# Transposing raw x before its layer norm, and pairing two triples of score banks, in a pre-LN transformer block

## The chip, the cores and the metric

The kernel runs on one core of a Trainium2 chip. The metric is the device time of one execution in microseconds (us). The engines are TensorE (PE in the profile, its weight loads PEld), VectorE (DVE), ScalarE (ACT), GpSimd (POOL) and the DMA queue that SyncE (SP) feeds.

## The reference

One block for 2048 tokens of width 640, in bf16, with 32 heads of 20 and a gated feed-forward of 1728:

```
def _layernorm(x, axis=-1, eps=1e-5):
    m = jnp.mean(x, axis=axis, keepdims=True)
    v = jnp.var(x, axis=axis, keepdims=True)
    return (x - m) / jnp.sqrt(v + eps)
...
qkv = (x @ wqkv) split into q, k, v of 32 heads x 20
p = softmax(q k^T * 20 ** -0.5);  A_ref = (p v) @ wo
B_ref = (gelu(x @ w_gate) * (x @ w_up)) @ w_down
h = x + A_ref(_layernorm(x));  out = h + B_ref(_layernorm(h))
```

## The kernel before

**Planner.** The program is a list of operations made by `op(engine, instructions, duration, priority, ...)`. `Sched.schedule` plays them through with the given durations and fixes the order of each engine's instructions: among the operations that are ready, the lowest priority number goes first. PSUM has eight banks; an operation that starts a chain acquires one of an allowed set, and the one that empties it releases it. The tuples at the head of the file (QK_LEAD, PE_AGE, SD_AGE and others) steer the choice for PE, one number for each slot. Most instructions carry line 450, that of a helper.

**First stage.** x comes in four loads of 512 tokens, then the weights of Q, K and V. Statistics for tiles 0 to 10 (128 tokens each) come from bn_stats on DVE (`ln_stats`), for tiles 11 to 15 from sums on ACT (`act_stats`). `ln_rsqrt` makes 1/std, `ln_apply` on DVE the normalised tile, PE transposes it (L675), and ACT or DVE copies it to `xnT` (L681, L684). From `xnT` come K and Q of the first 128 channels (`proj_k(0)`, `proj_q(0, 0)`, products at L758, copies at L795 and L800), and V (`proj_v`, L907, copies at L917). The maximum of |K| (`km`, L792) scales a bound on the scores (`sel0`, `q_bound0`), which Q carries as an extra row. Scores can be formed from then on. The other channels of K, Q and V are projected as background in the first slots (copies at L803).

**Attention.** Queries are cut into chunks of 512, 256 (five times) and 128 (twice): `CHUNKS`. A slot is one PSUM bank of output: one group of four heads for 512 queries, two groups for 256, four for 128. That is 32 slots: 0 to 7 for chunk 0, four each for chunks 1 to 5, two each for chunks 6 and 7. A slot has 64 score tiles of 128 x 512 numbers. Most go through the exponential on ACT, in units of two or three tiles: scores in banks 0 to 2, then in 3 and 4, and so on in turn, each unit one ACT instruction of 1024 or 1536 columns into `pts` or the part of `rege` called `pts2`. D_SLOT[s] x 4 tiles of slot s go to DVE: a quad is four conversions from PSUM (L992) and four steps over 2048 columns, whose four terms PE adds up in the P x V product; SUMS says how many pairs of terms DVE adds itself instead. A DVE tile either rides in the third bank of a unit (D_RING says how often; that unit then has two ACT tiles) or has a score matmul of its own and one of the background banks. P x V accumulates in bank 6. DVE copies it out at a slot's end (`epilogue`). Where PE would be idle the planner adds products with zeros (`pad`, `warm`).

**Background.** `post(c)` (output projection, layer norm, feed-forward of chunk c) runs beside the attention of the later chunks, in the banks of `BG` (7 and 5 before); its evacuations are L1285, L1373, L1379, L1390 and L1410. What is left after the last exponential, with chunk 7's own `post`, is the tail.

## Time and profile before

| what | us |
|---|---|
| median of three runs | 867.64 (867.41 to 868.66) |
| span of the profiled execution | 866.0 |
| its own time | not given apart from the span |
| first exponential starts | 32.84 |
| last exponential ends | about 841.5 |

The span runs from the first to the last instruction of the core; a run's time is a little longer. In the page's rows "xN" counts instructions, "busy" is the time in which an engine has any of them in work, and the mean duration of one contains its overlap with the next. The rows that matter are shown in the prediction.

### The profile page before, as it was taken

The page shows a single profiled execution, that of the slowest core. Times are in us where ns is not written, and L with a number is a line of the kernel's source. Part 1 is how long each engine was busy: PE and PEld are TensorE (multiplying, and loading weights), DVE is VectorE, ACT ScalarE, POOL GpSimd, SP SyncE. Part 2 cuts the span into 40 slices and gives each one's busy share as a digit, 9 for nine tenths or more (in the row PEclk, how much of TensorE's full clock was granted, in tenths as well). Part 3 has the DMA queues.
Part 4 walks back from the last instruction along what each step waited for, and adds up shares of the span by engine and source line. Part 5 has one row for each costly group of instructions (what it writes and reads, how often), then busy time and mean ns, then how long its engine had stood idle before and what let it go on. Part 6 is the DMA issues. An engine that isn't in the chain of part 4 may idle for free.

```text
span 866.0 us, 35545 instructions
## 1 busy us (share of the span) xinstructions
PE 838.5 (97%) x16215; PEld 420.4 (49%) x16215; DVE 750.4 (87%) x1372; ACT 838.4 (97%) x806; POOL 89.6 (10%) x268
## 2 busy tenths in 40 slices
...
GB/s 274 81 47 61 29 76 47 59 61 92 58 16 60 160 147 80 16 18 36 53 42 16 36 8 61 5 35 17 49 19 24 58 12 27 20 47 11 2 18 17
DMA packets 50173, 43.19 MB, mean 50 GB/s; under 512 B 21316, under 2 KB 44640, under 8 KB 50024
## 3 DMA queue, kind: packets, MB, share of 16 engines
...
q8 instruction: 127, 2.08, 1.0%
q14 instruction: 22, 0.18, 0.1%
...
## 4 chain that ended last, share of the span: by engine, by line
ACT 51%; PE 39%; DVE 8%; issue 1%
ACT pts L450 35%; ACT rege L450 15%; PE ps L1081 11%; PE ps L450 10%; PE ps L753 9%; PE ps L758 3%; DVE qt_all L450 2%; DVE rege L450 2%; PE ps L907 1%; PE ps L1336 1%; DVE rege L992 1%; DVE qt_all L992 1%; PE ps L1405 1%; ACT qt_all L450 1%; PE ps L675 1%
## 5 line engine op out<-in xcount | busy, mean ns | idle before, releaser
L450 ACT ACTIVATE pts<-ps 128x1024 bf16<-128x1024 f32 (+1 forms) x496 | 558.5, 1240 | 2.8 <-PE ps L1081 2.2
L1081 PE MATMUL ps<-qt_all,kt_all 32*128 32x256 bf16 (+2 forms) x4096 | 304.0, 273 | 11.5 <-ACT pts L450 5.6
L450 ACT ACTIVATE rege<-ps 128x1024 bf16<-128x1024 f32 (+1 forms) x222 | 248.3, 1199 | 0.7 <-PE ps L1081 0.3
L1081 PEld LDWEIGHTS ps<-qt_all,kt_all 32*128 32x128 bf16 x4096 | 103.2, 92 | 202.8 <-ACT pts L450 90.6
L992 DVE TENSOR_SCALAR rege<-ps 128x512 int16<-128x512 f32 x220 | 148.5, 684 | 20.0 <-PE ps L1081 18.6
L450 PE MATMUL ps<-rege,v_all 128*21 128x256 bf16 (+2 forms) x2197 | 139.3, 286 | 0.5 <-DVE rege L450 0.5
L450 PE MATMUL ps<-pts,v_all 128*21 128x256 bf16 (+2 forms) x2403 | 124.8, 273 | 1.0 <-DVE osb L450 0.8
L753 PE MATMUL ps<-rege,regw 128*32 128x256 bf16 (+1 forms) x2600 | 120.5, 296 | 1.6 <-DVE rege L992 0.5
L992 DVE TENSOR_SCALAR qt_all<-ps 128x512 int16<-128x512 f32 x128 | 86.7, 683 | 11.0 <-PE ps L1081 10.2
L450 DVE TENSOR_SCALAR rege<-rege 128x2048 int16<-128x2048 int16 x141 | 94.5, 687 | 1.5 <-PE ps L450 0.8
L753 PEld LDWEIGHTS ps<-rege,regw 128*32 128x32 bf16 x2600 | 60.4, 96 | 34.6 <-issue 20.1
L450 PEld LDWEIGHTS ps<-rege,v_all 128*21 128x21 bf16 x2197 | 54.4, 91 | 41.6 <-issue 26.1
L450 PEld LDWEIGHTS ps<-pts,v_all 128*21 128x21 bf16 x2403 | 56.6, 91 | 26.0 <-issue 19.2
L450 DVE TENSOR_SCALAR qt_all<-qt_all 128x2048 int16<-128x2048 int16 (+4 forms) x113 | 65.4, 589 | 3.0 <-ACT qt_all L450 1.0
L753 PE MATMUL ps<-regw,rege 128*32 128x320 bf16 x1296 | 67.4, 301 | 0.3 <-DVE rege L992 0.3
L758 PE MATMUL ps<-regw 128*128 128x512 bf16 (+2 forms) x215 | 59.6, 368 | 0.4
L450 PE MATMUL ps<-qt_all,v_all 128*21 128x256 bf16 (+1 forms) x1264 | 56.5, 264 | 0.8 <-DVE qt_all L450 0.8
L450 DVE TENSOR_SCALAR qt_all<-rege 128x2048 int16<-128x2048 int16 x80 | 53.8, 684 | 1.6 <-PE ps L450 1.2
L450 POOL TENSOR_SCALAR rn<-rc 128x16 int32<-128x16 int32 x22 | 7.0, 317 | 461.7 <-DMA rc<-sums 461.6
L1390 DVE TENSOR_TENSOR rege<-rege,ps 128x512 bf16<-128x512 bf16 (+2 forms) x53 | 35.0, 661 | 13.0 <-PE ps L753 6.6
L1336 PE MATMUL ps<-rege,regw 128*128 128x128 bf16 (+1 forms) x420 | 40.9, 238 | 0.0
L753 PEld LDWEIGHTS ps<-regw,rege 128*32 128x32 bf16 x1296 | 30.0, 96 | 18.3 <-issue 10.8
...
## 6 DMA issues: line engine op xcount, KB each, us to landing
...
```

The costliest lines, as they stand in the source:

```text
L450: return lambda eng: getattr(eng, method)(*args, **kwargs)
L675: op("pe", lambda eng, a=a: eng.transpose(bank16(bk, D)[:, 128 * a:128 * a + 128], src[:, a * 128:(a + 1) * 128], ident[:]), 0.055, prio, ...
L753: return [lambda eng, j=j: eng.matmul(out()[32 * j:32 * j + 32], l[:, 32 * j:32 * j + 32], r, start=start, stop=stop, tile_position=(0, 32 ...
L758: fn = col4(lambda: bank(bk, n), l, r, k == 0, k == len(steps) - 1) if col else lambda eng, l=l, r=r, k=k: eng.matmul(bank(bk, n), l, r, s ...
L907: w_readers.append(op("pe", lambda eng, i=i, kt=kt, a=a: eng.matmul(bank(bk)[:, i * w:i * w + w], xnT[:, a, kt * 128:(kt + 1) * 128], wv[: ...
L992: d_ops.append(op("dve", lambda eng: eng.tensor_scalar(v[:, 512 * h:512 * h + 512], bank(b), EXP_MUL, -32000.0, ALU.mult, ALU.max), c_dve( ...
L1081: return lambda eng: eng.matmul(out()[:, kk * nq:(kk + 1) * nq], kt_all[32 * j:32 * j + 32, g, kt * 128:(kt + 1) * 128], qt_all[32 * j:32 ...
L1336: lambda eng, a=a, f=f, fi=fi: eng.matmul(bank(bk)[:, fi * nq:(fi + 1) * nq], w[:, a, F0[f]:F0[f] + 128], hnT[:, a, 128 * tb:128 * tb + nq ...
L1390: hdone.append(op("dve", lambda eng, bu=bu, fv=fv, w=w: eng.tensor_tensor(fv, fv, bank(bu, w), ALU.mult), c_dve(w), p, reads=[ku] + hkeys( ...
L1405: f == NF - 1) if cl else lambda eng, f=f, o=o, bk=bk, w0=w0, w1=w1: eng.matmul(
```

## The change

**First stage.** x is transposed as it arrives (`xT`, which has a column of ones behind each 128 tokens). The mean is taken out of the weights: a matmul with ones gives the column sums, ACT copies them scaled by 1/640, POOL or DVE (CM_DVE) subtracts them (`center`); the weights are loaded in slices, the first 128 columns of K and of Q between the sets of x. 1/std is put on the products. For the first channels of K and Q (`proj_t0`) the product is formed with tokens on the partitions, scaled there by `rs`, and transposed back; the other K and Q products are multiplied on DVE with a broadcast of 1/std (`make_r`, buffers `rb`), V with `rs`. Tiles outside BN get their mean and squares from a Gram product of the transposed tile: the last column and the diagonal. `act_stats` and the normalised tiles of the first stage are gone.

**Attention.** Chunks 2 to 5 (slots 12 to 27) pair banks 0 to 2 with banks 3 to 5. P x V takes bank 6 or 7 in turn, and BG is what is left of 7, 6, 5 and 4. DVE tiles of the next slot may come up to eight ahead (AHEAD). D_SLOT, SUMS, D_RING, D_SPAN and D_FIRST get other numbers. The planner's costs for changing the PE's tiling are given for each pair of modes, and its tuples for each slot are other numbers.

```diff
-D_SLOT = (1,) + (3,) * 26 + (2, 3, 3, 0, 0,)
-SUMS = (0,) + (1,) * 4 + (2, 2, 0, 0, 1, 0,) + (1,) * 3 + (0, 1, 1, 2, 3, 1, 0, 1, 1, 0, 2, 2, 1, 0, 1, 0, 3, 0,)
+D_SLOT = (2,) + (3,) * 27 + (4, 2, 0, 0,)
+SUMS = (2, 1, 1, 1,) + (0,) * 5 + (1, 0, 1, 1,) + (0,) * 8 + (2, 1, 0, 0, 1, 1,) + (0,) * 5
...
+TOK_DVE = ((False, 0, 0), (False, 1, 0), (False, 1, 1), (False, 3, 0), (True, 0, 0), (True, 1, 1), (True, 2, 0), (True, 2, 1), (True, 3, 0), (True, 3, 1))
+CM_HOLD = 1
+CM_DVE = (('wk', 2), ('wk', 4), ('wq', 4), ('wv', 1), ('wv', 2))
...
-D_RING = (9,) * 4 + (6, 6,) + (9,) * 6 + (6,) * 16 + (12,) + (6,) * 3
-D_FIRST = 0
-D_SPAN = (16,) + (18,) * 13 + (17,) + (18,) * 4 + (19,) * 4 + (18,) * 7 + (17, 17,)
-D0 = 8
-P33 = ()
...
+D_RING = (12, 9, 9, 9, 3,) + (9,) * 4 + (6, 6, 6, 12, 24,) + (12,) * 9 + (9, 12, 24, 9, 9, 9, 6, 3, 9,)
...
+PVB, BGB = (6, 7), (7, 6, 5, 4)
+D_FIRST = (8,) + (0,) * 7 + (-2,) + (0,) * 10 + (2, 0, 0, -2, 2,) + (0,) * 6 + (1, 1,)
+AHEAD = 2
+D_SPAN = (15, 18, 17,) + (18,) * 9 + (17, 16, 18, 17, 17, 17, 18, 17, 18, 17, 17, 17, 19, 17, 17, 17, 18, 22, 22, 15,)
+P33 = (2, 3, 4, 5)
...
+LORD = ('x0', 'k', 'x1', 'q', 'x2', 'x3')
+RAW_DVE = (7, 9)
...
+BN = (0, 1, 2, 3, 7, 8, 10, 11, 12, 15)
...
-GROUPS = ((0, 4), (4, 7), (11, 5))
+GROUPS = ((0, 4), (4, 8), (12, 4))
...
+        def center(w, lo, hi, cm, ckeys, lkey, parts, prio):
...
+                    op("pe", lambda eng, a=a, a0=a0, bk=bk, n_=n_: eng.matmul(
+                        bank(bk, n_), one[:, 0:1].to_broadcast([128, 128]), w[:, a, lo + a0:lo + a0 + n_], start=a == 0, stop=a == NA - 1),
+                       c_mm(n_), prio, mode="full", reads=[lkey, "one"], writes=[key], acq=[bk] if a == 0 else [])
...
+                eng = "dve" if wkey in CM_DVE else POOL
+                op(eng, I("tensor_tensor", w[:, :, lo + a0:lo + a1], w[:, :, lo + a0:lo + a1],
+                          cm[:, a0:a1].unsqueeze(1).to_broadcast([128, NA, a1 - a0]), ALU.subtract),
...
+        center(wqk, D, D + 128, cm_t0[:, 0:128], [("bs", j) for j in range(4)], "lk0", [(0, 128, ("wk", 0))], P_K0)
+        center(wqk, 0, 128, cm_t0[:, 128:256], [("bs", j) for j in range(4)], "lq0", [(0, 128, ("wq", 0))], P_K0)
+        for t in range(NT):
+            transposes(x_sb[:, t, :], [f"x{t // 4}"], xT[:, :, t, 0:128], ("xnT", t), ALLB, P_TR, "dve" if t in RAW_DVE else "act")
+            e_ops.append(len(sc.ops) - 2)
...
+                    op("pe", lambda eng, i=i, t=t, a=a, bk=bk: eng.matmul(
+                        bank(bk)[:, 129 * i:129 * i + 129], xT[:, a, t, 0:128], xT[:, a, t, 0:129], start=a == 0, stop=a == NA - 1),
+                       c_mm(129), P_GR, mode="full", reads=[("xnT", t), "xones"], writes=[key], acq=[bk] if i == a == 0 else [])
...
+                op("dve", lambda eng, i=i, t=t, bk=bk: eng.scalar_tensor_tensor(
+                    out=junk[t % 8], in0=bank(bk)[:, 129 * i:129 * i + 128], scalar=1.0, in1=ident[:], op0=ALU.mult, op1=ALU.mult,
+                    accum_out=ssq[:, t:t + 1]), 0.25, P_RS, reads=[key, "ident"], writes=[("junk", t % 8), ("ssq", t)], rel=[bk] if i == n - 1 else [])
+        for t in BN:
+            ln_stats(x_sb[:, t, :], t, [f"x{t // 4}"], P_RS)
         for t0, n in GROUPS:
-            if (t0, n) == AG:
-                act_stats(t0, n)
-            else:
-                for t in range(t0, t0 + n):
-                    ln_stats(x_sb[:, t, :], t, [f"x{t // 4}"], P_BG)
-            ln_rsqrt(t0, n, P_RS, sqrt=True)
...
-                e_ops.append(ln_apply("dve", x_sb[:, t, :], xn_p[:, t % 4, :], ("xnp", t % 4), t, [f"x{t // 4}"], P_PRO))
...
+            op("act", I("activation", sl(mu), mv[:, t0:t0 + n, 1], ACT.Sqrt, bias=eps[:]), 0.2, 1, reads=k("mv") + ["eps"], writes=k("mu"))
+            v(I("reciprocal", sl(rs), sl(mu)), k("mu"), k("rs"))
+
+        def make_r():
...
+                        op("pe", lambda eng, i=i, src=src, name=name, bk=bk: eng.matmul(
+                            bank(bk)[:, 128 * i:128 * i + 128], src.to_broadcast([128, 128]), ident[:], start=name == "rhi", stop=name == "rlo"),
+                           c_mm(128), P_R, mode="full", reads=[name, "ident"], writes=[key], acq=[bk] if i == 0 and name == "rhi" else [])
+                fn = lambda eng, c=c, bk=bk: eng.activation(rb[c], bank(bk), ACT.Copy) if R_ENG == "act" else eng.tensor_copy(rb[c], bank(bk))
+                op(R_ENG, fn, c_act(512) if R_ENG == "act" else c_dve(512), P_R, reads=[key],
+                   writes=[("R", c)], rel=[bk], after=tuple(e_ops[0:8]) if c < 3 else ())
...
+            w_readers.append(op("dve", lambda eng: eng.tensor_tensor(dst, bank(bk), rb[c], ALU.mult), c_dve(512), prio,
+                                reads=[key, ("R", c)] + rb_home[c], writes=[dkey], rel=[bk], after=after))
+        def proj_t0(col, c, dst, dkey, banks, prio):
+            isk = col > 0
+            buf, home = (ktok, ("da", 0)) if isk else (qtok, "ka")
+            for p in range(2):
...
+                if (isk, c, p) in TOK_DVE:
+                    op("dve", lambda eng, bk=bk, ts=ts: eng.tensor_tensor(
+                        buf[:, ts[0]:ts[0] + 2, :], bank(bk, 256).rearrange("p (t s) -> p t s", t=2),
+                        rs[:, ts[0]:ts[0] + 2].unsqueeze(2).to_broadcast([128, 2, 128]), ALU.mult), c_dve(256), prio,
...
+                op("pe", lambda eng, i=i, t=t: eng.transpose(bank16(bk, 512)[:, 128 * i:128 * i + 128], buf[:, t, :], ident[:]), 0.055, prio - 0.005,
+                   mode="full", reads=[("tok", isk, t), "ident", home], writes=[key], acq=[bk] if i == 0 else [])
...
+            rv = rs[:, kts[0]:kts[0] + n].unsqueeze(2).unsqueeze(3).to_broadcast([128, n, 4 * (g1 - g0), DH])
+            w_readers.append(op("dve", lambda eng: eng.tensor_tensor(dst, src(), rv, ALU.mult), c_dve(n * w), prio,
+                                reads=[key] + [("rs", kt) for kt in kts], writes=wr, rel=[bk], after=after))
...
-            want = min(nd, (k[0] - first) * nd // (D_SPAN[s_] if isinstance(D_SPAN, tuple) else D_SPAN) + 1) if k[0] >= first and nd else 0
...
+                for t, k in ((s_, in_slot[s_]), (s_ + 1, in_slot[s_] - n_units[s_])):
+                    if t == len(slots) or not d_rem[t]:
+                        continue
+                    nd = 4 * len(d_kb[t])
+                    i = d_used[t]
+                    if k >= d_first[t] + i * D_SPAN[t] / nd - 1e-6 and i < nd and (t == s_ or i < 4 * AHEAD):
+                        xd = d_rem[t].pop(0)
+                        d_used[t] += 1
+                        ring[-1] = n == 3 and (i + 1) * D_RING[t] // nd > i * D_RING[t] // nd
+                    break
+                n -= ring[-1]
...
+            if not pv_ops:
+                pv_ops.append(Bank(*PVB))
+            bk = pv_ops[0]
...
-        BG = [tuple(b for b in (7, 5, 4) if b not in PAT[c][0] + PAT[c][1]) for c in range(len(CHUNKS))]
+        BG = [tuple(b for b in BGB if b not in PAT[c][0] + PAT[c][1]) for c in range(len(CHUNKS))]
```

408 lines of the change are left out of this document (246 added, 162 removed).

## The prediction

> **What bounds the kernel now.** I read the page first, then the busy time by stage, then ScalarE's instructions by shape, then the chain of waits.
>
> ```profile
> span 866.0 us, 35545 instructions
> PE 838.5 (97%) x16215; PEld 420.4 (49%) x16215; DVE 750.4 (87%) x1372; ACT 838.4 (97%) x806; POOL 89.6 (10%) x268
> 0.00:32.80 32.80, 26.96 (x242) 20.37 (x242) 27.61 (x82) 25.25 (x47) 11.71 (x31) 0.95 0.53 193
> 32.80:228.00 195.20, 190.85 (x1733) 62.50 (x1732) 174.04 (x297) 193.97 (x181) 19.36 (x61) 1.00 0.22 63
> 529.70:629.00 99.30, 97.81 (x2449) 54.44 (x2444) 98.61 (x183) 99.15 (x95) 10.97 (x32) 1.00 0.11 30
> 730.30:841.50 111.20, 109.12 (x2888) 72.16 (x2880) 75.63 (x152) 109.98 (x103) 3.77 (x14) 1.00 0.10 22
> 841.50:866.00 24.50, 21.66 (x298) 18.14 (x295) 11.77 (x32) 7.93 (x15) 0.00 (x0) 1.00 0.04 15
> ```
>
> In the stage rows the busy times stand in the order PE, PEld, DVE, ACT, POOL. There are three stretches: a first stage of 32.8 us, the attention from 32.8 to 841.5 us in which ACT is busy nearly all the time, and 24.5 us of tail. PE looks as busy as ACT, but its score matmuls wait for ACT to give banks back, so ACT sets the pace:
>
> ```profile
> PEld ps L1081 <- ACT pts L450: 90.6, 281, 0.9
> ```
>
> What ACT does there, by shape:
>
> ```profile
> L450 ACT ACTIVATE pts<-ps 128x1024 bf16<-128x1024 f32 x300 | 308.2, 1073 | 0.9 <-PE ps L1081 0.6
> L450 ACT ACTIVATE pts<-ps 128x1536 bf16<-128x1536 f32 x196 | 293.0, 1495 | 1.9 <-PE ps L1081 1.6
> L450 ACT ACTIVATE rege<-ps 128x1024 bf16<-128x1024 f32 x154 | 156.8, 1070 | 0.1
> L450 ACT ACTIVATE rege<-ps 128x1536 bf16<-128x1536 f32 x68 | 101.4, 1491 | 0.6 <-PE ps L1081 0.3
> L450 ACT ACTIVATE qt_all<-qt_all 128x1024 f16<-128x1024 f16 x13 | 14.3, 1112 | 0.0
> L450 ACT ACT_TABLE_LOAD x8 | 10.3, 1283 | 0.9 <-PEq L1508 0.8
> L450 ACT ACTIVATE rege<-rege 128x2048 bf16<-128x2048 bf16 x4 | 7.4, 1902 | 0.0
> ```
>
> So 454 exponentials cover two score tiles (1024 columns) and 264 cover three: 1700 tiles. Their records overlap, so the price of one is its spacing, which the chain shows:
>
> ```profile
> 276.87 2.75 ACT rege L450 x3
> 279.62 5.44 ACT pts L450 x5
> ```
>
> The first row is three of 1024 columns, 0.917 us each. The second is three of 1024 and two of 1536, so one of 1536 takes (5.44 - 2.75) / 2 = 1.345, say 1.344. That is 0.427 us for a tile and 0.063 for an instruction. All exponentials: 454 x 0.917 + 264 x 1.344 = 771.1 us. The Gelu and Tanh rows, smaller shapes of both and four of the table loads add about 30 us. Of the 808.7 us from 32.8 to 841.5 some 8 us are left: gaps between exponentials, all that better timing could win.
>
> **Part 1: fewer and wider exponentials.** I worked through the loop over `units` with the diff's tuples: a slot has 64 tiles, 4 x D_SLOT of them go to DVE, and a unit takes 3, then 2 tiles (3, then 3 in slots 12 to 27), one less if a DVE tile rides in its third bank. With the old tuples the loop gives 454 and 264, as the rows show. With the new ones it gives 411 and 290: 1692 tiles, as D_SLOT sums to 89 instead of 87. Time: 411 x 0.917 + 290 x 1.344 = 766.6 us, that is **-4.5 us**: slot 0 gives 1.7, slots 1 to 11 0.4, slots 12 to 27 1.8, the last four 0.6. The 17 instructions fewer are 1.1 us of it, the 8 tiles 3.4. The wide third bank is thus mostly spent on the DVE tiles that ride (183 of 192 in slots 12 to 27, 49 before), not on wider exponentials.
>
> **Part 2: what DVE and PE pay for it.**
>
> ```profile
> L992 DVE TENSOR_SCALAR rege<-ps 128x512 int16<-128x512 f32 x220 | 148.5, 684 | 20.0 <-PE ps L1081 18.6
> L450 DVE TENSOR_SCALAR rege<-rege 128x2048 int16<-128x2048 int16 x141 | 94.5, 687 | 1.5 <-PE ps L450 0.8
> L450 DVE TENSOR_TENSOR qt_all<-qt_all 128x2048 bf16<-128x2048 bf16 x9 | 10.9, 1213 | 0.0
> 136.33 0.40 PE ps L1081 x3
> 140.16 0.97 PE ps L450 x16
> ```
>
> A DVE quad is four of the first and four of the second: 5.5 us. Two more: +11 us. SUMS asks for 13 pair sums instead of 28, each the third row: -18.2 us. DVE is eased by some 7 us over the attention. PE gets what the sums saved: 15 quads of P x V plus 3 x 2 for the new DVE quads, 21 quads at 0.24 us (the last row is 16 matmuls, four quads, in 0.97 us), +5 us. Against that 127 DVE tiles no longer need a score matmul and a bank of their own (348 - 95 = 253 before, 356 - 230 = 126 after). No row prices such a lone tile. The nearest is a whole unit (the L1081 row: three tiles at a time in 0.40 us), so it saves between nothing and 127 x 0.4 = 50 us; I take 0.2 us, 25 us over 16 slots. PE is eased too. As neither sets the end, I count only the gaps: of 8 us they could give back 4, and with a DVE that must now empty the third bank in time they could grow by 6. I take -1.
>
> **Part 3: the first stage.** This is the part with many terms.
>
> ```profile
> 11.63 0.16 DVE L450 RECIPROCAL rs<-sd 128x4 f32<-128x4 bf16 x1
> 30.51 0.16 DVE L450 TENSOR_REDUCE kd<-km 128x1 f32<-128x5 f32 x1
> 32.84 5.97 ACT pts L450 x5
> L450 DVE BATCH_NORM_STATS2 stats<-rege 128x6 f32<-128x320 bf16 x22 | 9.3, 455 | 0.0
> L450 DVE TENSOR_SCALAR rege<-rege,mu,rs 128x640 bf16<-128x640 bf16 x16 | 7.4, 497 | 0.3 <-PE ps L675 0.2
> L450 DVE BATCH_NORM_AGGREGATE mv<-stats 128x2 f32<-128x12 f32 x11 | 2.1, 194 | 0.1
> L684 DVE COPY regw<-ps 128x640 bf16<-128x640 bf16 x4 | 2.0, 489 | 0.4 <-PE ps L675 0.2
> L792 DVE TENSOR_REDUCE km<-ps 128x1 f32<-128x128 f32 x1 | 0.3, 280 | 0.0
> L1225 DVE CAST rege<-ps 128x256 bf16<-128x256 f32 x5 | 2.1, 418 | 0.0
> L681 ACT ACTIVATE regw<-ps 128x640 bf16<-128x640 bf16 x12 | 7.9, 718 | 1.0 <-PE ps L675 1.0
> L450 ACT ACTIVATE rege<-rege 128x640 bf16<-128x640 bf16 x10 | 7.3, 734 | 1.4 <-DMA rege<-in_A_x_dram 1.3
> ```
>
> The first exponential starts 2.3 us after the maximum over K is complete, and that link (kd, sel0, the bound, the first scores) stays. Ahead of it DVE is the busiest engine: 27.6 of 32.8 us, of which the first 6.5 us hold only fills. From DVE go 16 normalisations (7.4), one of eleven tiles of bn_stats with its aggregate (0.9), two of the four transpose copies (1.0), and the casts and small steps of `act_stats` and `ln_rsqrt` (about 12 at 0.15, 1.8): -11.1 busy. To it come six Gram diagonals (nearest row the 128-column reduction from PSUM, 0.28: 1.7), three means and nine small steps (0.15 each: 1.8), and seven scaled products of 256 columns (0.42: 2.9), with two steps for `make_r` (0.3): +6.7. Net -4.4 us busy. ACT loses ten passes for sums (7.3, and their accumulator reads) and gains two copies more (1.4), small products (about 1.5) and four copies of R (4 x 0.6): it stays below DVE. What follows the last statistics is one scaled product, a transpose and the reduction instead of normalise, transpose, copy, product and reduction, so it is no longer than before.
>
> The other bounds are arrivals. SP issues three loads more, all at the front; behind them in its queue come only the copies of Q and K, which wait for products, so nothing there is late. The last set of x comes behind two slices of 160 KB of weights, 0.4 us each at the 395 GB/s of the load, and the centring of those slices is a new step on POOL.
>
> ```profile
> GB/s 0 0 72 184 322 392 394 395 389 398 395 411 411 410 410 413 405 400 392 394 397 323 67 20 0 10 0 0 26 26 26 26 164 23 28 26 26 26 36 46
> L450 POOL MEMSET kt_all<- 128x1024 f32 x5 | 4.8, 952 | 0.3
> ```
>
> POOL subtracts 640 elements for each 128 columns. Its fill writes 1024 elements in 0.95 us; one stream instead of three puts the price between 0.6 us and three times that, 1.8. I take 1.7. By the first row (slices of 0.8 us) the first 0.8 MB, a set of x and a weight slice, have moved at about 5 us; landed near 6, with its column sums by 7.5, the slice is centred by 9 to 10 us. The first group's 1/std, which its products need too, was there at 11.8 us (the reciprocal above), so the step is covered; at twice the price it would be late by about 2 us for the first K product, but the last K product waits for the last statistics some ten microseconds later.
> The Trainium skill (GPSIMD Engine Reference, Specifications) says that GpSimd shares its SBUF interfaces with VectorE and contends with DVE instructions in a two-port mode or with two SBUF inputs, which speaks against this step. Its elementwise table gives 4497 ns for an add over 2048 fp32, by which an estimate for 640 is 1.4 us. No run here shows a two-input POOL instruction of this size beside DVE. By that estimate the sum is unchanged; a long stall by that rule is the third rival.
>
> I take the first exponential at 28.4 us, **-4.4 us**, between -1 (latencies eat it) and -7 (DVE idles less, too). After it, R may need up to four ACT slots of 0.5 us among the exponentials: between 0 and +2, I take +0.5, since ACT has idle time ahead of the first scores. Five subtractions on DVE (0.4 to 0.7 us each, 2.7 in all, bounded by the 640- and 1536-column prices above) and all V copies come after the first exponential, where DVE was busy 174 of 195 us; that is in the second rival.
>
> **Part 4: the tail.** Its code is the same; PE is busy 21.66 of its 24.5 us, so background work (projection, feed-forward) that is left over at 841.5 us adds to it nearly one to one: the 2.8 us that PE idles and a little more below, a whole chain of a 256-token chunk (8 us, by 28 evacuations' matmuls of 1.2 us, a quarter of them) above. Between -3 and +8, I take 0.
>
> Sum: -4.5 - 1 - 4.4 + 0.5 = **-9.4 us** on a span of 866.0, so 856.6. The page gives no other time for its execution; the runs' median lies 1.6 us above the span (867.41 to 868.66 for the three), which I keep: **858.2 us**.
>
> **The rivals.**
>
> *One background bank.* In slots 12 to 27 the pair of triples leaves banks 6 and 7, one of which holds P x V, so background chains get one bank where they had two. The evacuations of such chains in slots 20 to 23:
>
> ```profile
> L1373 DVE TENSOR_SCALAR rege<-ps 128x512 bf16<-128x512 f32 (+1 forms) x12 | 7.9, 658 | 0.0
> L1390 DVE TENSOR_TENSOR rege<-rege,ps 128x512 bf16<-128x512 bf16 (+1 forms) x8 | 5.3, 659 | 0.0
> L1410 DVE TENSOR_TENSOR rege<-ps,rege 128x320 bf16<-128x320 f32 x4 | 1.9, 481 | 0.0
> L1285 DVE TENSOR_TENSOR rege<-ps,rege 128x320 bf16<-128x320 f32 x4 | 1.9, 468 | 0.0
> ```
>
> ```profile
> 493.48 0.99 PE ps L753 x32
> ```
>
> These 28 evacuations in 99.3 us leave 3.5 us for one turn of a single bank. A turn is some 1.2 us of matmuls (32 in 0.99 us by the last row, forty for a bank), 0.66 of evacuation, up to 0.6 behind the DVE instruction in service, and two score units of 0.4 in between: 3.3 us. It decides from 3.5 us. At 4 us some 28 x 4 x 0.5 = 56 us of turns would be owed at slot 28; the last four slots, with two banks, could catch up perhaps two thirds, and 18 us go to the tail: 876. For it: DVE busy 98.6 of 99.3 us there. Against: the DVE tiles, which used the same banks, now ride.
>
> *DVE full in slots 0 to 3.* One quad more in slot 0 (5.5), the sums of slot 0 (2.4), the five subtractions (2.7): 10.6 us on a stage 89% busy. If half turns into ACT gaps: +5, 863.
>
> *No shorter first stage.* POOL's subtraction, slowed beside DVE, or the later x holds the last K product: 862.6, the gain of part 1 and the gaps alone.
>
> *The eased PE gets background work done early,* so that the tail shrinks by 3 and the gaps by 4 instead of 1: 852.
>
> **How the numbers follow.** Forecast 0.46, one bank 0.10, DVE full 0.18, first stage 0.12, eased PE 0.14. The forecast's own range is 854 to 862. To hold 8 in 10 the range takes in the rivals on the fast side and the two milder ones: 850.5 to 866.5; left out are the one-bank case and the double failures. A measurement can tell about 0.2% (1.7 us). Faster by more: 0.46 + 0.17 + 0.10 + 0.14, 0.87 rounded down to 0.86; slower 0.10; the rest 0.04.
>
> **What would show it.** First exponential between 27 and 30 us; 411 and 290 exponentials; gaps of ACT in the attention of 4 to 10 us; pair sums 13; a tail of 24 to 25 us. A first exponential after 31.5, a tail over 28, or gaps over 13 us would prove a step wrong.

## The result and the profile after

The changed kernel takes **880.96 us** (median of 4 runs, 879.58 to 883.4) against 867.52 us for the kernel before on the same chip (866.51 to 868.66): 1.0158 times, 95% interval 1.0139 to 1.0176. The forecast was 858.2 us, in a range that ended at 866.5. The profiled execution is the longest of the four (883.4 us, span 881.7); the two executions with a granted clock of 0.998 took 879.6 and 880.2 us, the two with 0.994, this one among them, 881.8 and 883.4. The head of its page:

```profile
span 881.7 us, 36087 instructions
PE 835.4 (95%) x16434; PEld 421.7 (48%) x16447; DVE 744.9 (84%) x1377; ACT 832.1 (94%) x785; POOL 108.1 (12%) x279
```

The same five stretches as in the prediction (columns: PE, PEld, DVE, ACT, POOL busy, granted clock, DMA share, GB/s):

```profile
0.00:29.50 29.50, 25.00 (x327) 21.56 (x329) 25.10 (x83) 24.33 (x43) 20.11 (x40) 1.00 0.68 210
29.50:235.90 206.40, 199.34 (x1746) 66.32 (x1743) 182.90 (x308) 192.84 (x182) 27.79 (x64) 0.99 0.24 63
540.90:641.20 100.30, 91.75 (x2275) 48.93 (x2270) 99.03 (x184) 100.17 (x93) 10.63 (x32) 1.00 0.10 22
737.40:850.90 113.50, 109.78 (x3099) 72.94 (x3100) 74.55 (x157) 111.48 (x102) 5.41 (x14) 1.00 0.10 20
850.90:881.70 30.80, 28.32 (x378) 24.57 (x376) 18.31 (x46) 8.04 (x15) 0.00 (x0) 1.00 0.05 18
```

The first stage is shorter, as forecast. Three things are new. In the second row ACT is idle for 13.6 of 206.4 us, where it was idle for 1.2 of 195.2. In the third row ACT is full and PE is idle for 8.5 us of 100.3 (1.5 of 99.3 before). In the last row there is more left to do after the exponentials, with PE busy 28.3 us instead of 21.7. The exponentials themselves, by shape:

```profile
L461 ACT ACTIVATE pts<-ps 128x1024 bf16<-128x1024 f32 x292 | 305.0, 1100 | 5.9 <-PE ps L1229 4.6 <-PE ps L1174 0.8
L461 ACT ACTIVATE pts<-ps 128x1536 bf16<-128x1536 f32 x202 | 302.0, 1527 | 5.0 <-PE ps L1174 3.7 <-PE ps L1229 0.8
L461 ACT ACTIVATE rege<-ps 128x1536 bf16<-128x1536 f32 x88 | 133.3, 1530 | 2.8 <-PE ps L1229 2.7
L461 ACT ACTIVATE rege<-ps 128x1024 bf16<-128x1024 f32 x119 | 126.6, 1099 | 7.9 <-PE ps L1174 5.8 <-PE ps L1229 2.1
```

These are 411 and 290, as forecast. The last numbers of each row are ACT's idle time before them and what ended it: scores (L1229) that came late, or stood behind P x V (L1174) in PE's order.

Where the 15.7 us between the two spans came from, in the forecast's terms. The gaps are the spacing of each exponential's end from the end before it, less 0.917 or 1.344 us, summed; the last exponential ends at 849.9 us (841.5 before).

| term | forecast | measured |
|---|---|---|
| first exponential (32.84 to 29.54 us) | -4.4 | -3.3 |
| fewer, wider exponentials | -4.5 | -4.5 |
| gaps between exponentials (8.9 to 26.0 us) | -1 | +17.1 |
| other ACT work between first and last exponential | +0.5 | -1.0 |
| tail after the last exponential (24.5 to 31.8 us) | 0 | +7.3 |
| sum | -9.4 | +15.6 |

Of the 17.1 us of gaps, 13.9 lie before 140 us (0.6 to 14.5) and 5.6 in slot 10, where PE waited for a piece of w_gate; elsewhere they fell. That wait, and then the early gaps, which begin with DVE (timelines of the changed kernel; columns: start, length, engine, instruction, and in brackets the idle time before it and what ended it):

```profile
299.90 1.04 PE L842 MATMUL ps<-rege,regw 128*32 128x512 bf16 x8 [2.76 <-DMA regw<-in_B_w_gate_dram]
```

```profile
25.78 1.62 DVE L461 TENSOR_SCALAR sel<-sel,kd 128x4 bf16<-128x4 bf16 x2
28.08 3.17 DVE L461 TENSOR_TENSOR regw<-regw,wda 128x1200 bf16<-128x1200 bf16 x2
31.18 3.28 DVE L461 TENSOR_TENSOR regw<-regw,bsum 128x640 bf16<-128x640 bf16 x2
34.37 0.48 DVE L461 TENSOR_TENSOR regw<-regw,on 128x640 bf16<-128x640 bf16 x1
34.77 1.21 DVE L1023 TENSOR_TENSOR v_all<-ps,rs 128x480 bf16<-128x480 f32 x2
51.02 0.22 DVE L461 TENSOR_SCALAR sel<-sel,kd 128x32 bf16<-128x32 bf16 x1
```

```profile
25.97 2.75 POOL L461 TENSOR_TENSOR regw<-regw,bsum 128x640 bf16<-128x640 bf16 x2
28.68 5.43 POOL L461 TENSOR_TENSOR regw<-regw,on 128x640 bf16<-128x640 bf16 x3
```

A subtraction of 640 elements takes DVE 1.64 us while POOL subtracts too, and 0.48 us at 34.37 us, when POOL has finished. The first copy of V therefore comes at 34.77 us, and what is queued behind it in PE's fixed order starves ACT:

```profile
36.04 0.98 PE L1174 MATMUL ps<-pts,v_all 128*21 128x512 bf16 x8 [2.26 <-DVE v_all L1023]
51.30 0.39 PE L979 MATMUL ps<-regw,sel 128*32 128x512 bf16 x1 [0.90 <-DVE sel L461]
```

```profile
37.60 1.02 ACT L461 ACTIVATE rege<-ps 128x1024 bf16<-128x1024 f32 x1 [2.09 <-PE ps L1229]
40.12 1.45 ACT L461 ACTIVATE rege<-ps 128x1536 bf16<-128x1536 f32 x1 [1.50 <-PE ps L1229]
52.62 1.94 ACT L461 ACTIVATE rege<-ps 128x1024 bf16<-128x1024 f32 x2 [4.28 <-PE ps L1174]
```

A part of both losses is PE's clock. Behind the wait that ends at 36.04 us and behind the one for w_gate it was granted at half (third number from the end). The first two rows are the changed kernel; the third is c3, an experiment below whose PE waits in the same way before 36.04 us:

```profile
36.20:39.60 3.40, 3.40 (x15) 0.69 (x7) 0.38 (x1) 1.02 (x1) 0.00 (x0) 0.51 0.51 168
299.00:305.80 6.80, 5.90 (x70) 1.84 (x70) 1.38 (x2) 2.43 (x3) 0.47 (x3) 0.50 0.43 114
36.20:39.60 3.40, 3.40 (x24) 1.02 (x17) 1.08 (x2) 2.09 (x2) 0.00 (x0) 1.00 0.50 168
```

At half the clock PE gets through 15 matmuls in these 3.4 us, in c3 through 24. The gaps before 140 us are 14.5 us in the changed kernel and 12.9 us in c3, so nearly all of the early gaps stand without the half clock. How much of the 5.6 us in slot 10 it makes is open.

### The profile page after: what moved, and what is told of

Read it like the earlier page. It is cut to its first block, busy times and chain, and to the rows that moved or that the text cites. A ratio compares the mean times of both kernels' runs of the same rounds, so it can differ in the third digit from the quotient of the medians.

```text
span 881.7 us, 36087 instructions
## 1 busy us (share of the span) xinstructions
PE 835.4 (95%) x16434; PEld 421.7 (48%) x16447; DVE 744.9 (84%) x1377; ACT 832.1 (94%) x785; POOL 108.1 (12%) x279
## 4 chain that ended last, share of the span: by engine, by line
ACT 43%; PE 33%; DVE 20%; DMA 2%; issue 1%; POOL 1%; SPq 0%; POOLq 0%
ACT pts L461 30%; ACT rege L461 13%; PE ps L1229 9%; PE ps L1174 7%; DVE qt_all L461 5%; PE ps L842 5%; DVE rege L461 3%; PE ps L871 3%; DVE rege L1110 3%; DVE qt_all L1110 3%; PE ps L1015 2%; PE ps L1484 2%; DMA regw<-in_B_w_gate_dram 2%; PE ps L1553 1%; DVE rege L1521 1%; DVE regw L461 1%
## 5 line engine op out<-in xcount | busy, mean ns | idle before, releaser
L1229 PE MATMUL ps<-qt_all,kt_all 32*128 32x256 bf16 (+2 forms) x4096 | 292.6, 273 | 21.3 <-ACT pts L461 9.3
L461 ACT ACTIVATE rege<-ps 128x1024 bf16<-128x1024 f32 (+1 forms) x207 | 246.5, 1282 | 10.7 <-PE ps L1174 5.8
L1229 PEld LDWEIGHTS ps<-qt_all,kt_all 32*128 32x128 bf16 x4096 | 95.4, 92 | 211.3 <-ACT pts L461 110.6
L1110 DVE TENSOR_SCALAR rege<-ps 128x512 int16<-128x512 f32 x224 | 151.3, 683 | 32.6 <-PE ps L1229 31.6
L1174 PE MATMUL ps<-rege,v_all 128*21 128x256 bf16 (+2 forms) x2242 | 139.0, 288 | 0.4 <-DVE rege L461 0.3
L1174 PE MATMUL ps<-pts,v_all 128*21 128x256 bf16 (+2 forms) x2406 | 122.2, 274 | 2.5 <-DVE v_all L1023 2.3
L461 DVE TENSOR_SCALAR rege<-rege 128x2048 int16<-128x2048 int16 x145 | 97.4, 687 | 2.8 <-PE ps L1174 2.2
L1110 DVE TENSOR_SCALAR qt_all<-ps 128x512 int16<-128x512 f32 x132 | 88.8, 682 | 10.7 <-PE ps L1229 10.5
L1174 PEld LDWEIGHTS ps<-rege,v_all 128*21 128x21 bf16 x2242 | 53.4, 91 | 40.9 <-issue 21.8
L1174 PEld LDWEIGHTS ps<-pts,v_all 128*21 128x21 bf16 x2406 | 57.4, 92 | 29.4 <-issue 19.0
L461 DVE TENSOR_SCALAR qt_all<-qt_all 128x2048 int16<-128x2048 int16 (+2 forms) x116 | 66.9, 589 | 2.0 <-ACT qt_all L461 1.2
L842 PE MATMUL ps<-regw,rege 128*32 128x320 bf16 x1296 | 62.6, 301 | 2.2 <-DVE rege L1558 1.2
L1174 PE MATMUL ps<-qt_all,v_all 128*21 128x256 bf16 (+1 forms) x1368 | 60.7, 265 | 1.1 <-DVE qt_all L461 1.1
L1538 DVE TENSOR_TENSOR rege<-rege,ps 128x512 bf16<-128x512 bf16 (+2 forms) x53 | 34.9, 660 | 21.5 <-PE ps L842 9.8
L871 PE MATMUL ps<-regw 128*128 128x512 bf16 x175 | 52.1, 390 | 0.8 <-DVE rege L1110 0.5
L1558 DVE TENSOR_TENSOR rege<-ps,rege 128x320 bf16<-128x320 f32 (+2 forms) x32 | 15.5, 486 | 27.4 <-PE ps L1553 15.2
```

The lines of the kernel that those rows point to most:

```text
L461: return lambda eng: getattr(eng, method)(*args, **kwargs)
L842: return [lambda eng, j=j: eng.matmul(out()[32 * j:32 * j + 32], l[:, 32 * j:32 * j + 32], r, start=start, stop=stop, tile_position=(0, 32 ...
L871: w_readers.append(op("pe", lambda eng, a=a: eng.matmul(bank(bk).rearrange("p (t s) -> p t s", s=128), wqk[:, a, col + 128 * t:col + 128 * ...
L1110: d_ops.append(op("dve", lambda eng: eng.tensor_scalar(v[:, 512 * h:512 * h + 512], bank(b), EXP_MUL, -32000.0, ALU.mult, ALU.max), c_dve( ...
L1174: fns.append(lambda eng, o=nq * gs.index(g), j=j, kt=kt, g=g, pt=pt, kk=kk, st=(s_, j) not in pv_start: eng.matmul(bank(bk)[32 * j:32 * j ...
L1229: return lambda eng: eng.matmul(out()[:, kk * nq:(kk + 1) * nq], kt_all[32 * j:32 * j + 32, g, kt * 128:(kt + 1) * 128], qt_all[32 * j:32 ...
```

## PE's time, counted whole

Here every moment of PE is sorted by what moved its end on: scores, P x V, all other products, filler (products with zeros and others of no use, which only keep it busy during the attention), idle. Idle counts from the start of the span, so 2.9 us of it before and 3.7 us after the change lie ahead of PE's first instruction; but for some 2.5 to 2.9 us behind its last one the kinds add up to the span. "Other" holds projections, feed-forward and the first stage, with the products of zeros that run there (11.2 us before, 10.4 us after).

| kernel | other | scores | P x V | filler | idle | time, us |
|---|---|---|---|---|---|---|
| before | 350.3 | 260.0 | 203.1 | 25.1 | 24.7 | 867.5 |
| changed | 358.0 | 252.1 | 208.1 | 17.1 | 43.9 | 881.0 |
| before, order with hop 0.31 (n2) | 349.7 | 267.7 | 204.5 | 24.4 | 27.4 | 879.4 |
| changed, no pairs of triples (c3) | 356.0 | 264.1 | 208.4 | 18.1 | 31.0 | 882.9 |
| changed, no centring (a5) | 353.0 | 251.6 | 210.4 | 21.9 | 40.4 | 880.7 |
| changed, neither (f1) | 352.4 | 264.7 | 207.3 | 17.4 | 26.0 | 872.7 |

PE was idle for 3% of the kernel before. Net, the change adds 7.7 us of other products and 5.0 us of P x V, saves 7.9 us of scores, and adds 19.2 us of idle time, of which 8.0 us take the place of filler. So PE's work grows by 4.8 us (813.4 to 818.2), and what it does not work, idle and filler together, by 11.2 us (49.8 to 61.0). In c3 the second sum is 49.1 us, as before the change, and the work 828.5 us: there the whole loss is work.

## The experiments

Behind each measured time stand its ratio to the kernel before and the 95% interval of that ratio. In the expectations "gaps" are those of ACT, "slots 12 to 27" are chunks 2 to 5. All ratios are to the kernel before in the same session. A change of any planned duration makes the plan anew, so all kernels below also differ from each other in the order of instructions; how much that alone is worth is measured in the second group.

**Is it the subtractions? (a1, a2, a3) And the wait for w_gate? (b1)**

```diff
a1: -CM_DVE = (('wk', 2), ('wk', 4), ('wq', 4), ('wv', 1), ('wv', 2))
a1: +CM_DVE = ()
a2: +CM_DVE = all of wk1..4, wq1..4, wv0..2
a3: -(0.061 + NA * (a1 - a0) * 0.00055) if eng == "dve" else ...
a3: +1.6 if eng == "dve" else ...
b1: -sem="wp", lat=3.4
b1: +sem="wp", lat=4.5
```

> The changed kernel with all eleven later subtractions of the column means on POOL (CM_DVE empty); the plan is made anew. Theory (two-stream subtractions of DVE and POOL slow each other: on DVE 1.64 us beside POOL against 0.48 us with POOL idle, five of them some 5 us later than planned at the start of the attention): the gaps of ACT before 130 us, 14.8 us in the changed kernel over the kernel before, fall by 6 to 10 us, and the time by as much: 871 to 875. Rival (DVE is full in slots 0 to 3 by its other work: the extra quad of slot 0, its two pair sums, the V copies): DVE loses only 2.7 us of planned work, the gaps fall by 0 to 3 us, 878 to 881. Second rival (POOL alone takes 1.4 us for 640 elements, so V comes later): gaps as now or larger, 881 or more.

> The changed kernel with all eleven later subtractions on DVE; POOL keeps only the first slice of K and of Q. Theory (collision): with POOL idle each costs DVE 0.48 us for 640 elements, all eleven some 6 us, less than the 6.6 us and more that the five take beside POOL now; the gaps of ACT before 130 us fall by 5 to 10 us, 871 to 876. Rival (DVE is full in slots 0 to 3): DVE has 3 us more of planned work there, the gaps grow by 1 to 3 us, 882 to 884.

> The changed kernel, in which the plan counts each of the five DVE subtractions at 1.6 us instead of 0.41 to 0.72 us, as the trace of the changed kernel has them; the same instructions, in another order. If the loss comes of the plan's surprise (instructions queued in a fixed order behind late ones), the gaps of ACT before 130 us fall by 5 to 10 us, 871 to 876. If it comes of the time itself that DVE loses to the collision, they fall by 0 to 3 us, 878 to 881.

> The changed kernel, in which the plan gives each piece of the late weight loads 4.5 us instead of 3.4 us to land, so that the first matmuls on w_gate are planned after its arrival (299.86 us in the changed kernel, where PE waited 2.76 us for it and ACT lost 5.6 us in slot 10). Theory: the gaps of slot 10 fall to under 1.5 us and the time by 4 to 5 us: 876 to 877. Rival (the lost time is made up by a later stage, since the feed-forward then starts later and leaves more for the tail): the gaps of slot 10 go, the time changes by less than 2 us: 879 to 882.

Measured: a1 891.19 us (1.0270, 1.0254 to 1.0285), a2 892.5 us (1.0285, 1.0258 to 1.0312), a3 889.64 us (1.0254, 1.0237 to 1.0271), b1 889.15 us (1.0244, 1.0227 to 1.0261). All are slower than the changed kernel. No expectation of time held but the open one of a1's second rival, "881 or more", and that not for its reason: V's first copy comes at 31.0 us, earlier than the 34.8 us of the changed kernel. The gaps before 140 us are 14.2 (a1), 21.2 (a2) and 15.3 us (a3): subtractions no longer collide in a1 and a2, and the gaps stay. On POOL alone the eleven subtractions run from 24.3 to 41.7 us and hold back the second K; on DVE alone they end at 32.6 us, and the third and fourth copies of V come at 39.3 and 58.7 us (51.2 and 55.9 in the changed kernel). In a2 the clock was granted at 0.50 from 32.9 to 50.0 us, so its 21.2 us are not those of the subtractions' place alone; a1 had the full clock throughout. So the collision as such is not what the early gaps hang on.

In b1 the gaps of slot 10 are gone (5.6 to 0.0 us), as the theory said, and the last exponential ends 4 us earlier, at 845.9 us. But the tail is 41.7 us long. The same exchange shows in a1 and a3: last exponential at 847.4 and 846.1, tail 42.0 and 41.9 us. What ACT wins, PE owes at the end, and more: 2.5 to 4.0 us against 10. In all three PE has 5 to 9 us more of idle time and filler than in the changed kernel (66.2 to 69.6 us), with its work nearly unchanged; how much of that is the new order's is not shown.

**How much is the order alone worth? (n1, n2, and later m1, m2, m3)**

```diff
-D_LAT = 0.3
+D_LAT = 0.31   # n1: changed kernel; n2: kernel before; 0.29 in m1 (before) and m3 (changed), 0.33 in m2 (before)
```

> The changed kernel, in which the plan counts the hop after a DVE sum or term as 0.31 instead of 0.30 us (D_LAT). The instructions are the same and their order on PE, DVE and ACT differs in many places, so it tells what another order alone is worth. Theory (each order of the changed kernel pays for the collision at the start and for a feed-forward that comes late; the four altered orders took 889 to 893): 878 to 892, away from 881 by several us, with the gaps of ACT and the tail moving against each other (the last exponential earlier, the tail longer, or the other way). Rival (the losses are those of the parts, the order is worth nothing): 879 to 883.

> The kernel before with the same altered hop (0.31 instead of 0.30 us). Theory (its order is as fitted to its plan as that of the changed kernel, or it has slack): if the order matters as much here, 874 to 882; if the kernel before has slack in its background work, 866 to 871. The second is taken as likelier by the theory that the changed kernel lost slack by its pairs of triples.

> The kernel before with the plan's hop after a DVE sum or term at 0.29 instead of 0.30 us: the same instructions in another order. Theory (the order of the kernel before is fitted to the chip, and any other costs some ten us): 874 to 884, PE's time on scores 264 to 269 us in all instead of 260, tail over 28 us. Rival (the order with 0.31 us was an unlucky one): 866 to 872.

> The kernel before with that hop at 0.33 us. Theory as for 0.29 us: 874 to 884 and 264 to 269 us of PE on scores. Rival: 866 to 872.

> The changed kernel with that hop at 0.29 us. Theory (the parts of the change cost PE some 5 us more than they save it, in any order): 881 to 890, PE idle in slots 12 to 27 at 22 to 28 us, early gaps of ACT 12 to 21 us. Rival (the changed kernel has orders as good as the old one): below 876.

| order | kernel before, us | changed kernel, us |
|---|---|---|
| own (0.30) | 867.5 | 881.0 |
| 0.29 | 883.28 (1.0180, 1.0163 to 1.0197) | 887.01 (1.0229, 1.0204 to 1.0253) |
| 0.31 | 879.41 (1.0133, 1.0118 to 1.0148) | 885.43 (1.0197, 1.0180 to 1.0214) |
| 0.33 | 871.07 (1.0061, 1.0016 to 1.0106) | |

This was the surprise. A hundredth of a microsecond in one planned latency (the plan's wait after each DVE term), with the same instructions, costs the kernel before 11.6 and 15.7 us. The case taken as likelier for n2, 866 to 871, missed and the other held; n1, m1 and m3 came within the times of their theories, m2 within that of its rival. In n1 gaps and tail both grew (17.0 us before 140 us, 34.6 us), where its theory had them move against each other. Both kernels are best in the order they came with, and at 0.29 and 0.31 the old one by more. With 0.31 PE spends 267.7 us on scores instead of 260.0, and the tail is 31.8 us, as long as the changed kernel's:

```profile
844.80:876.60 31.80, 27.14 (x366) 22.14 (x363) 16.59 (x43) 11.23 (x18) 0.00 (x0) 1.00 0.04 12
```

So a tail of 32 us says nothing about the change by itself. Between altered orders the change costs 6.0 us (0.31) and 3.7 us (0.29); with the own orders 13.4. The orders of the kernel before spread over 16 us, so the share of the order cannot be given closer than this: the change is slower in each of the three comparisons, and more than half of the 13.4 us may be lost fit.

**Which part does it? (c1, d1, c3)**

```diff
c1 (changed kernel, old attention): tuples D_SLOT, SUMS, D_RING, D_SPAN, QK_LEAD, PE_AGE, SD_AGE, SD_ROW of before, AHEAD = 0, D_FIRST = (8,) + (0,) * 31
c1: -P33 = (2, 3, 4, 5)
c1: +P33 = ()
c1: +PVB, BGB = (6,), (7, 5, 4)
d1 (kernel before, new attention): the diff's units, P x V banks, tuples and scheduler; none of its first stage
c3 (changed kernel): -P33 = (2, 3, 4, 5)
c3:                  +P33 = ()
```

> The new first stage with the attention of before: the old tuples for the DVE tiles, sums, rings, spans, leads and ages, no pair of triples, P x V in bank 6 and background in banks 7 and 5 (one function for the units, which gives the old counts). Theory (the pairs of triples with fewer background banks make the late tail, the collision the early gaps): first exponential at 29.5 us, early gaps of 5 to 12 us over the kernel before, tail 24 to 27, exponentials 4.5 us dearer: 869 to 876. Rival (the new first stage alone does the harm, as background starts behind and stays so): tail of 30 us or more, 880 to 890. Second rival (the first stage is a gain by itself): 863 to 866.

> The kernel before with the attention of the changed kernel (its units, tuples, pairs of triples, P x V in bank 6 or 7, plan's price of a mode switch) and the old first stage. Theory (early gaps belong to the new first stage; the new attention saves ACT 4.5 us and loses the fit of the old order and one background bank): first exponential 32 to 33 us, gaps before 140 us under 3 us, PE idle in slots 12 to 27 over 15 us, tail over 28 us, 870 to 880. Rival (the new attention gains what the forecast said): tail 24 to 25 us, 861 to 865.

> The changed kernel with pairs of three and two in every chunk (P33 empty), all other tuples as changed, so that background has banks again and some DVE tiles need a place of their own. Theory (the pairs of triples cost PE idle time and save it score matmuls): PE idle between 336 and 737 us falls from 23.1 us to 8 to 13, PE's time on scores in the attention rises from 251.5 us to 260 to 268, and the time stays within 876 to 886. Rival (idle time there is not the banks'): idle stays over 18 us. The early gaps before 140 us (14.5 us) stay by both, as slots 0 to 3 are not touched.

Measured: c1 888.51 us (1.0237, 1.0222 to 1.0253), d1 890.29 us (1.0250, 1.0234 to 1.0265), c3 882.89 us (1.0187, 1.0157 to 1.0216). Each half of the change alone is slower than both together, by less than the orders of the kernel before differ among themselves. The time of c1 is that of its first rival, 880 to 890; that of d1 lies above both of its ranges. c1 has 20.3 us of gaps before 236 us although its attention is the old one; the longest stands behind 5.6 us of postponed K and Q products:

```profile
147.11 2.37 ACT L461 ACTIVATE pts<-ps 128x1024 bf16<-128x1024 f32 x2 [11.39 <-PE ps L1229]
```

So they come with the first stage, as the altered orders of the kernel before have 2.3 to 3.5 us there. But d1, with the old first stage, has 10.8 us of gaps before 140 us, where under 3 were expected, so not all of them do: three of d1's, 2.6, 3.2 and 3.6 us, end where PE comes back to the scores after P x V. As expected, PE is idle for 25.3 us in d1's slots 12 to 27.

PE's idle time sorts the kernels cleanly. Slots 12 to 27 of the kernel before, of the changed kernel and of c3 (second column: length of the window, third: PE busy):

```profile
330.00:730.00 400.00, 392.37 (x9274) 206.84 (x9266) 369.11 (x650) 399.07 (x370) 44.03 (x128) 1.00 0.12 31
```

```profile
336.00:737.00 401.00, 377.91 (x9142) 195.75 (x9145) 357.70 (x636) 400.21 (x359) 42.54 (x128) 1.00 0.12 29
```

```profile
336.00:737.00 401.00, 391.66 (x9229) 203.46 (x9227) 357.99 (x641) 398.96 (x387) 42.22 (x128) 1.00 0.11 28
```

That is 7.6, 23.1 and 9.3 us. c3 also shows the other side: the scores take PE 264.1 us instead of 252.1. The pairs of triples save 12 us there and lose 14 us of idle time, so c3 and the changed kernel end almost together, as the theory said. (Without the pairs the units are narrower again: c3, f1, g1 and g2 have 507 and 226 exponentials instead of 411 and 290, 2.0 us dearer by the spacings.)

**One background bank, or a full DVE? (x3, h)**

```diff
x3 (kernel before): -bd = Bank(*BG[slots[xd[0]][0]])
x3:                 +bd = Bank(*((5,) if slots[xd[0]][0] in (2, 3, 4, 5) else BG[slots[xd[0]][0]]))
x3:                 -post(c, ALLB if tail else BG[c + 1], tail)
x3:                 +post(c, ALLB if tail else BGX[c + 1], tail)   # BGX is (7,) for chunks 2 to 5
h (changed kernel): +w_ = 256 if i > 1 and d_t[e] > 2 * len(d_a[e]) and slots[raw[0][0]][0] in P33 else 2048
h:                  -op("dve", I("tensor_scalar", a, v, 0.25, off, ...
h:                  +op("dve", I("tensor_scalar", a[:, 0:w_], v[:, 0:w_], 0.25, off, ...
```

> The kernel before with one background bank in chunks 2 to 5: bank 7 alone for the projection and feed-forward of those chunks, bank 5 alone for DVE tiles without a place in a unit; the pairs of three and two stay. PE's idle time between 330 and 730 us is 7.7 us in the kernel before and 8.6 us in its order with the other hop, 23.1 us in the changed kernel (slots 12 to 27). Theory (one bank of background starves PE): 14 to 24 us idle there. Rival (PE idles there for lack of ready work, whatever the banks): 7 to 11 us. The time by either is that of another order, 872 to 890, and by the theory at the upper end.

> The changed kernel, in which the third and fourth term of each DVE quad in chunks 2 to 5 are written for 256 columns instead of 2048 (the rest of these tiles keeps older values), so that DVE has some 50 us less to do there (96 instructions of 0.69 us become about 0.15), while the banks, PE's matmuls and ACT's exponentials stay. Rival DVE full: chunk 2 to 5 come out 10 us or more earlier against the kernel, the tail goes to 25 us or less, 870 to 876. Rival one background bank: a turn of the bank (3.6 us in the middle) loses at most the 0.3 us that an evacuation waits for DVE, the tail stays at 29 us or more, 878 to 884.

Measured: x3 890.42 us (1.0259, 1.0244 to 1.0274), h 883.58 us (1.0180, 1.0165 to 1.0195). The windows of x3 and of h:

```profile
330.00:730.00 400.00, 379.73 (x8649) 192.91 (x8650) 355.85 (x621) 390.29 (x363) 43.38 (x128) 1.00 0.12 28
```

```profile
336.00:737.00 401.00, 378.25 (x9238) 198.97 (x9235) 322.21 (x644) 398.25 (x358) 37.50 (x128) 1.00 0.12 28
```

The kernel before with one background bank idles PE for 20.3 us (its other orders: 8.6, 10.1 and 10.2). Between 420 and 441 us ACT has long gaps there, but PE is idle for only 1.0 of the 20.3 us:

```profile
420.00:441.00 21.00, 20.03 (x442) 10.46 (x444) 17.66 (x38) 13.55 (x13) 0.90 (x2) 1.00 0.16 43
```

So the idle time is not theirs. In h DVE has 35 us less to do, and PE still idles 22.7 us. It brings chunk 2 out 35 us earlier (592 instead of 627 us), the first half of what the rival expected, but the tail stays at 32.3 us and the time at 883.6. With every kernel measured the same line divides them: 7.2 to 10.7 us of idle time where background has two banks or shares two with DVE tiles, 20.3 to 27.1 us where it has one. The bank is the cause of this idle time; a full DVE is not. In the changed kernel it is no net loss: the pairs of triples that take the bank save about as much in scores (c3).

**Are there two limits, one behind the other? (a5, f1)**

```diff
 def center(...):
+    for _, _, wkey in parts: sc.lw[wkey] = sc.lw[lkey]
+    return
f1 also: P33 = ()
```

> The changed kernel without the centring of the weights: no column sums, no subtractions on POOL or DVE (the products use the raw weights); everything else stays. Theory of the subtractions (they hold V and the K and Q of the next groups back): gaps of ACT before 140 us fall from 14.5 us to under 6. Rival (work that the new first stage put off, V and the second K and Q, has no room on PE and DVE in slots 0 to 3, whatever holds it): 9 us or more stay. PE has 4 to 5 us less work by either (column sums of 1920 columns in five parts), so the end comes 4 to 12 us earlier: 870 to 878 by the theory, 876 to 884 by the rival.

> The changed kernel without the centring of the weights (raw weights in the products) and with pairs of three and two in every chunk. Each alone left the time as it was (880.7 and 882.9 against 881.0 us). Theory (two limits one behind the other: early gaps of ACT, and PE idle for one background bank; taking one away hands the time to the other): PE idle in slots 12 to 27 at 8 to 12 us as without the pairs, gaps before 140 us at 5 us as without centring, last exponential at 837 to 843, tail 29 to 33 us, 866 to 874. Rival (PE's own work is the only limit, which falls by 5 us at most): 876 to 881.

Measured: a5 880.71 us (1.0146, 1.0130 to 1.0161), f1 872.74 us (1.0057, 1.0042 to 1.0072). Without centring V is there in time, ahead of the first exponential at 29.2 us:

```profile
22.15 0.63 DVE L1026 TENSOR_TENSOR v_all<-ps,rs 128x480 bf16<-128x480 f32 x1
25.60 0.65 DVE L1026 TENSOR_TENSOR v_all<-ps,rs 128x480 bf16<-128x480 f32 x1
27.85 0.65 DVE L1026 TENSOR_TENSOR v_all<-ps,rs 128x480 bf16<-128x480 f32 x1
```

The gaps before 140 us fall from 14.5 to 5.2 us and the last exponential comes 11.6 us earlier, at 838.3 us. The theory had the gaps right and the rival the time, which stays, because 10.0 us of it go into the tail (a5, then f1; the window is the tail):

```profile
838.30:880.10 41.80, 39.25 (x481) 33.22 (x479) 23.08 (x54) 8.89 (x16) 0.00 (x0) 1.00 0.05 17
```

```profile
846.60:870.30 23.70, 20.90 (x282) 17.60 (x274) 11.14 (x31) 7.79 (x14) 0.00 (x0) 1.00 0.05 15
```

f1, with the banks back as well, has a tail of 23.8 us and gains 8.2 us on the changed kernel, in the range that the theory gave, though its last exponential at 846.6 us is later than the 837 to 843 expected and its tail shorter than the 29 to 33. The likely reading is that either limit alone hides what taking the other away would bring. As each of these kernels was measured in one order, and the changed kernel's own three differ by 6.0 us, the 8.2 us do not prove it. Even f1, which leaves the centring out, is not faster than the kernel before.

**Is the centring merely late? (g1, g2)**

```diff
-CM_DVE = (('wk', 2), ('wk', 4), ('wq', 4), ('wv', 1), ('wv', 2))
+CM_DVE = ()
-P_CM = 1.5
+P_CM = 1.3    # g2: 1.46
-P33 = (2, 3, 4, 5)
+P33 = ()
```

> The changed kernel with pairs of three and two in every chunk, all centring on POOL, and its column sums planned ahead of the first stage's other work (P_CM 1.3 instead of 1.5). Theory (lateness): POOL starts on V's weights at about 16 us instead of 24, is through by some 35 us, the gaps of ACT before 140 us fall from 14.5 us to 4 to 8, PE idles 9 to 12 us in slots 12 to 27, tail 24 to 33, 868 to 877. Rival (the work itself, PE's column sums and the later V): gaps stay over 11 us, 879 to 886. The first exponential may come up to 2 us later by either.

> The same with the column sums at priority 1.46, behind the transposes and Gram products and ahead of the products of K and Q. Theory: as for the other, with the first exponential nearer to 29.5 us and the gaps before 140 us between 5 and 10 us; 868 to 878. Rival: gaps over 11 us, 879 to 886.

Measured: g1 888.77 us (1.0236, 1.0221 to 1.0252), g2 889.6 us (1.0238, 1.0219 to 1.0257). Both times missed: the gaps before 140 us fell only to 8.7 us in both (between the two cases of g1, within the theory of g2), and the first exponential came at 40.4 and 39.7 us, ten us later, which neither had. The timeline of g1 shows why, DVE first and then POOL:

```profile
18.81 0.44 DVE L461 BATCH_NORM_STATS2 stats<-rege 128x6 f32<-128x320 bf16 x1
19.25 1.41 DVE L461 TENSOR_SCALAR regw<-regw 128x512 int16<-128x512 int16 x1
20.70 4.70 DVE L461 TENSOR_TENSOR mv<-mv 128x3 f32<-128x3 f32 x3
25.31 1.50 DVE L461 TENSOR_TENSOR mv<-ssq,mv 128x3 f32<-128x3 f32 x3
26.73 2.71 DVE L461 TENSOR_SCALAR mv<-mv 128x3 f32<-128x3 f32 x3
29.36 0.19 DVE L461 RECIPROCAL rs<-mu 128x8 f32<-128x8 f32 x1
```

```profile
18.81 6.56 POOL L461 TENSOR_TENSOR regw<-regw,wda 128x800 bf16<-128x800 bf16 x3 [1.31 <-ACT wda L761]
25.33 5.43 POOL L461 TENSOR_TENSOR regw<-regw,bsum 128x640 bf16<-128x640 bf16 x4
```

Nine steps on up to three numbers per partition, which take some 0.15 us each in the changed kernel, fill 8.7 us here, because POOL subtracts at the time. They stand between the statistics and 1/std. PE, busy for 3.1 of the 5.8 us from 18.8 us on, then has the clock granted at 0.50 from 24.6 to 34.9 us, which adds to the delay. So centring earlier on POOL blocks the path to the first exponential, and centring later delays V and the second K; no place tried for it was free. A version faster than the kernel before was not found.

## Why the prediction was wrong, step by step

**What bounds the kernel.** The failed step is the sentence that PE "looks as busy as ACT, but its score matmuls wait for ACT to give banks back, so ACT sets the pace". The row is right, the conclusion is not: PE was idle for 24.7 of 866.0 us (49.8 with the filler), so two engines bound the kernel together, and no sum for PE stands behind the gaps (-1) and the tail (0), the two terms that came out at +17.1 and +7.3. The a5 run shows it most plainly: a last exponential 11.6 us earlier is paid back by 10.0 us of tail. In a1, a3 and b1 one that is 2.5 to 4.0 us earlier goes with 10 us more of tail.

**Part 1** held: 411 and 290 exponentials, and the spacing by shape as before.

**Part 2** failed in the gaps, +17.1 us for a forecast of -1 and a bound of +6. The saving of 25 us on PE's scores, from 127 lone tiles at 0.2 us, was mis-sized: 7.9 us against the old order, 0.06 us a tile, and 12.0 against c3, which by the loop over the units has 89 lone tiles more (215), 0.13 us a tile. The price of P x V, +5 us, was exact. What PE gets besides, 7.7 us net of column sums (4.3 us), Gram products, 1/std rows and the like, was in no term: part 3 counted DVE and ACT alone. Leaving the centring out took 5.0 us of it away.

**Part 3** came close to the first exponential, 29.5 us instead of 28.4, but by two errors against each other. The maximum over K was complete earlier (kd at 25.51 us, where 28.4 less the 2.3 us of the link gives 26.1), and the link behind it took 4.0 us. What held it was ACT: the four copies of R, for which the forecast had ACT slots after the first exponential, stand before it, with a table load behind them. The changed kernel, then a2:

```profile
26.03 2.19 ACT L828 ACTIVATE rege<-ps 128x512 f32<-128x512 f32 x4
28.24 1.28 ACT L461 ACT_TABLE_LOAD   x1
28.20 0.59 PE L1229 MATMUL ps<-qt_all,kt_all 32*128 32x512 bf16 x5 [0.69 <-DVE qt_all L1003]
```

```profile
27.53 0.59 PE L1229 MATMUL ps<-qt_all,kt_all 32*128 32x512 bf16 x5
29.56 2.37 ACT L461 ACTIVATE pts<-ps 128x1536 bf16<-128x1536 f32 x2
```

In the kernel before, the first exponential started 0.44 us after the first scores (32.40 us), here 1.34 us after them, and in a2, where the scores come 0.67 us earlier, no sooner.

The price of the five DVE subtractions, "0.4 to 0.7 us each", was too low by two to four times in four of the five: 1.6 us, as the rows at 28.08 and 31.18 us show, and 0.48 for the one with POOL at rest; 6.9 us together instead of 2.7. The same collision met the second of the two scalings in the row at 25.78 us: some 1.3 us instead of the 0.22 us that the same shape took at 51.02 us. It delayed the first scores, but by a2 not the first exponential. The rule of the Trainium skill that was weighed there (GPSIMD Engine Reference, Specifications: shared SBUF interfaces, contention with DVE in a two-port mode or with two SBUF inputs) agrees with the rows of the subtractions, which have two SBUF inputs, and with the steps of g1 that have two; in which mode the scalings ran no row shows. The estimate of 1.4 us from that page's elementwise table is what POOL took for 640 elements, 1.40 us; the 1.7 us of the forecast was too much. But the rival drawn from it placed the stall ahead of the last K product. It came behind it, and the a1 run shows that the gaps stay when the subtractions no longer collide. The step of this part that failed most was "the step is covered": it looked at the first slices only, and let V, which now has to wait for its own centred weights, pass with "all V copies come after the first exponential". The copies of V went from 25.5, 32.3 and 33.5 us to 34.8, 35.3 and 51.2.

**Part 4**: the tail grew by 7.3 us, at the upper bound of 8. The bound was named for the reason that the row shows, left-over background (PE busy 28.3 of 30.8 us); but the kernel before in another order has the same tail, 31.8 us, so the growth is not shown to be the change's.

**The rivals.** *One background bank* was given 0.10, and its mechanism is the one that the runs bear out best. Its argument against itself, that DVE tiles no longer use those banks, was wrong as a reason: x3 gave the tiles their own bank and starved PE all the same. Its price was wrong too: 56 us of turns owed was too much, 15 us of PE idle time is what came, and the scores saved pay for most of it. *DVE full in slots 0 to 3* named the right place and about a third of the price (5 us for 13.9); what is late there is V and K, which wait for their centred weights, and not DVE's sum of work: in a1 DVE is rid of all five subtractions and the gaps stay at 14.2 us, in a5 nothing is centred and they fall to 5.2. *Eased PE* is refuted. What no rival held is that the change re-plans the whole order, and that the old order is a good one among its neighbours: with the span's terms all sized right, several us might still have been missed (13.4 us between the own orders, 6.0 and 3.7 between altered ones).

Open remain the share of the order in the 13.4 us, and with it the cause of that much of the loss, the 10.8 us of early gaps of d1, and why both halves alone (888.5 and 890.3 us) are slower than the whole.
